# Two reorderings in the start of a fused RWKV-6 attention and GELU MLP kernel

## The chip, the cores and the metric

The kernel runs on one core of one Trainium2 chip. The metric is the device time of one execution in microseconds (us). The kernel before was timed in six runs, with a median of 612.47 us and a spread from 611.44 to 615.05 us. One of these runs, with a time of 611.57 us, was also recorded by the hardware profiler, and all views of the profile come from it. The engines are called PE (TensorE), DVE (VectorE), ACT (ScalarE), POOL (GpSimd) and SP (SyncE, which only issues DMAs here). "L648" is line 648 of the kernel.

## The reference

The reference is a recurrent attention (RWKV-6 "Finch") followed by a two-layer MLP with an exact GELU. Everything is float32.

```python
B, H, S, D = 4, 8, 768, 48
for t in range(S):                                   # attention, per batch and head
    cur = einsum('bhd,bhe->bhde', u * k_t, v_t)
    y[:, :, t] = einsum('bhd,bhde->bhe', r_t, state + cur)
    state = w_t[..., None] * state + einsum('bhd,bhe->bhde', k_t, v_t)
x = y.transpose(0, 2, 1, 3).reshape(B * S, H * D)    # 3072 x 384
h = x @ w_in                                         # 384 x 2048
g = 0.5 * h * (1 + erf(h / sqrt(2)))
out = g @ w_out                                      # 2048 x 384
```

## The kernel before, in words

The 3072 tokens are cut into eight tiles of 384 tokens (two tiles for each batch entry). For each tile the kernel computes the attention, which leaves the transposed activations of the tile in a buffer `xT`, and then the MLP of that tile, which reads `xT`. The order of all instructions on every engine is the order in which the Python code emits them; no scheduler changes it.

**Attention as a generator.** `attention(x, unit)` is a Python generator. Each `yield` ends a *slot*, and the caller decides when the next slot is emitted. Time is cut into chunks of 64 tokens. The slots of tiles 0 and 1 are: products of decays (`tot_sb`, L371); the chunk's score matrix `a_sb`, level by level, with half block sizes 1, 2, 4, 8, 16 and 32 (PE products L402 into a PSUM tile `d`, DVE multiplications of r and k by decays L437, in place, and masked copies L447); the transposed k (L566, L568); the key-value products (`kv_ps`, L592); the state chain on DVE (`st`, L606 and L617); the products of the scores with v (`y_ps`, L630), closed by a tiny DVE copy called `fence` (L634), which waits for them; the products with the states, accumulated into `y_ps` (L648); and the copies of `y_ps` into `xT`. Level 1 is split in two slots: the first emits the level's PE products alone, and the next slot emits the diagonal's PE products (L402 with `kx` as an input, two calls), then L437, L447 and the diagonal's masked copies (L413). L437 of level 1 changes r and k, which the diagonal's products read, so it waits until they are done. PSUM tiles for this work rotate through three buffers with the tag "d"; the MLP has two others.

**Head pairs and units.** The eight heads are four pairs, 0 to 3. For tile 0 the attention is cut into two *units*, which run in turns: unit 0 has pairs 0 and 1, unit 1 has pairs 2 and 3. Each head has 48 dimensions, and a pair fills 2 x 48 of the 128 partitions of `xT`. Pair 3 is laid into the partitions that the others leave free: ACT copies it into `ysb` (L672), and six small DMAs (L676, three on SP's queue and three on ACT's) move it into `xT`. Pair 2 is copied by two DVE instructions (L669). Pairs 0 and 1 are copied by two ACT instructions followed by two DVE instructions (L656).

**The end of tile 0's attention.** By L892 both units have done everything up to their key-value products, and the list of units has been reversed, so that unit 1 comes first. Unit 1 then emits its last three slots (state chain; scores times v; states and copies), and after it unit 0 the same three. `keep_warm(n)` (L190) emits n bfloat16 matmuls of zeros between slots, and they write a buffer that nobody reads.

**Weights.** The weights come as 64-bit floats and are made float32 on the chip, in 16 pieces: eight of `w_in` (two of the 16 column blocks of 128 each) and eight of `w_out` (two blocks of 128 rows each). A piece costs two ACT instructions (L291, L292) and four DVE instructions (L303, L305, L306, L310). One `convert()` emits the DVE part of a piece, and the ACT part of a piece two later.

**The MLP of tile 0 beside the attention of tile 1.** The loop at L911 runs through the steps of `mlp(0)`. Step f (0 to 15) is one block of 128 columns of `w_in`: three PE instructions (L723, `h_ps`) and a GELU on ACT (L726). Steps 16 on are the second product (L857). Between the steps it emits a `convert()` at the steps 0, 2, 4, 6, 8, 10, 12, 14, 15, 17, 18, 20, 22 and 24, and after that one slot of tile 1's attention at each step in the list `place`. In that list, the entry 1 is level 1's products, the second entry is the slot with the diagonal and the rest of level 1, the third is level 2, and so on. Later tiles use other lists and are not touched.

Of the kernel before, what the change touches and what calls it, by code (L numbers as in the profile page):

```python
# [44 lines left out]
def kernel(  # L45
# [27 lines left out]
    NP = u.shape[1]  # L73
# [20 lines left out]
    def units_of(x):  # L94
        return NPART if x == 0 else 1
# [37 lines left out]
    def load(x, dma):  # L133

        if x >= NX:
            return
        loaded[x] = [None, None]
        for i in range(3):
            if i == 1:
                load_v(x, dma)  # L140
                yield
            t = bufs[x % 2 if i == 0 else 1]
            for j in range(3):
                a = i * ALL + j * ALL // 3
                dma.dma_start(out=t[:, a:a + ALL // 3], in_=rkw[x, :, a:a + ALL // 3])
                yield
# [40 lines left out]
    def keep_warm(n):  # L187
        t = ps.tile([128, BANK], F32, name="warm", tag="mm", bufs=2) if n else None
        for _ in range(n):
            nc.tensor.matmul(t, lhsT=zeros[:, 0:128], rhs=zeros, start=True, stop=True)  # L190
# [62 lines left out]
    def make_quarter_masks():  # L253
        make_fine()
        for (h, a), m_q in m_qs.items():
            nc.vector.tensor_tensor(out=quarter[h][a], in0=s_qs[h][:, 0:m_q.shape[1]], in1=m_q, op=ALU.is_equal)
# [22 lines left out]
    def convert():  # L279
        for _ in conversion():  # L280
            pass
# [32 lines left out]
    def attention(x, unit):  # L314
# [346 lines left out]
        for b in reversed(range(np_)):  # L661
            for q in reversed(range(Q)):
                pair = parts[b] * Q + q
                y = ys[b][:, :, q * N3 * C:(q + 1) * N3 * C].rearrange("p c (i t) -> p c i t", t=C)
                if pair < NJ:
                    for z in range(2):
                        s = slice(z * G, z * G + D)
                        copy = nc.vector.tensor_copy if x == 0 else nc.scalar.copy
                        copy(out=xT[s, pair, :].rearrange("p (i c t) -> p c i t", c=2, t=C), in_=y[s])  # L669
                    continue  # L670
                ysb = wk.tile([128, T], F32, name="ysb", bufs=1)
                nc.scalar.copy(out=ysb.rearrange("p (i c t) -> p c i t", c=2, t=C), in_=y)  # L672
                for z in range(2):
                    for j in range(NJ):
                        e = z * G + j * (G - D)
                        (nc.scalar if z * NJ + j > (2 if x == 0 else 3) else nc.sync).dma_start(out=xT[z * G + D:(z + 1) * G, j, :], in_=ysb[e:e + G - D, :])  # L676
# [12 lines left out]
    def w_sums():  # L689

        sums.extend(cv.tile([128, HF, HM], F32, name="t", tag="raw", bufs=AHEAD) for _ in range(4))
        s3_sb.append(cv.tile([128, HF, 128], F32, name="s3", tag="raw", bufs=AHEAD))
        for i, (x, y) in enumerate((((0, 1), (0, 0)), ((1, 1), 0), ((1, 1), (0, 1)), ((1, 0), 1))):
            for k in range(2):
                ks = slice(k * FG, (k + 1) * FG)
                nc.vector.tensor_sub(sums[i][:, ks], w_quarter(*x, k), sums[y][:, ks] if isinstance(y, int) else w_quarter(*y, k))
                yield
# [169 lines left out]


    units = [attention(0, unit) for unit in range(units_of(0))]
    second = load_second(nc.sync)  # L870
    shares = chain(weight_in(gate=True), second, weight_in(gate=True), weight_in(gate=True))
# [17 lines left out]
    for _ in shares:  # L889
        pass  # L890
    convert()
    for unit, warm in zip(units, ((1, 2, 1), (0, 0, 5))):  # L892
        for n in warm:
            next(unit)
            keep_warm(n)
    convert()
    slots = attention(1, 0)
    next(slots)

    for x in range(1, NX):

        place = [1, 2, 4, 7, 9, 11, 13, 15, 18, 20, 26, 32] if x == 1 else [1, 6, 8, 13, 15, 16, 18, 18, 20, 21]
        place_next = [38, 47] if x == 1 else [21, 24] if x % 2 == 0 else [25, 27]
        loads = load(x + 1, nc.scalar if x > 1 else nc.sync)

        times = range(20, 30) if x == 1 else (2, 3, 4, 5, 16, 17, 18, 19, 20, 21)
        following = attention(x + 1, 0) if x + 1 < NX else iter(())
        more = iter(())  # L910
        for step, _ in enumerate(mlp(x - 1)):  # L911
            if x == 1 and step == 2 * NF - 2:

                make_quarter_masks()
                more = w_sums()
            next(more, None)
            if x == 1 and step in (0, 2, 4, 6, 8, 10, 12, 14, 15, 17, 18, 20, 22, 24):
                convert()
            if step in times:
                next(loads, None)  # L920
            while place and place[0] <= step:
                place.pop(0)
                next(slots, None)
            while place_next and place_next[0] <= step:
                place_next.pop(0)
                next(following, None)
        for _ in slots:
            pass
        slots = following
# [62 lines left out]
```

## Time and profile before

| What | Value |
|---|---|
| Median of six runs | 612.47 us (611.44 to 615.05) |
| Profiled execution | 611.57 us |
| Its span, first to last instruction | 609.8 us |
| PE busy | 593.4 us (97%) |
| DVE busy | 448.6 us (74%) |
| ACT busy | 173.3 us (28%) |
| Mean granted PE clock | 0.994 |

The granted PE clock is given as a share of full speed. All stretches named below are in us from the span's start. The attention of tile 0 takes the first 46 us or so, and the MLP's first matmul (L723) starts at 46.38 us. From there to about 119 us, tile 1's attention, tile 0's MLP and the conversion of the weights run side by side. A busy PE is not a PE at its peak, and idle time of an engine that is not the bottleneck costs nothing.

### The profile page before, as it was taken

How to read it: one execution, taken by the hardware profiler on the slowest of the kernel's cores; microseconds unless marked ns; L12 is line 12 of the kernel's file. 1: busy time of each engine (PE TensorE's matmuls, PEld its weight loads, DVE VectorE, ACT ScalarE, POOL GpSimd, SP SyncE). 2: the span in 40 equal slices, each digit the busy share in tenths (PEclk: the TensorE clock that was granted, in tenths of full speed). 3: DMA queues.
4: the chain of work that ended last, by engine and by line, in shares of the span. 5: the costliest groups of instructions: out<-in, count | busy, mean ns of one | idle time of the engine just before them, and what ended most of it. 6: DMA issues, size and time to landing. Idle time of an engine off the chain costs nothing.

```text
span 609.8 us, 15812 instructions
## 1 busy us (share of the span) xinstructions
PE 593.4 (97%) x6917; PEld 447.0 (73%) x6935; DVE 448.6 (74%) x801; ACT 173.3 (28%) x389; POOL 8.4 (1%) x24
## 2 busy tenths in 40 slices
PE   7779999999999999999999999999999999999997
PEld 4555666656699578986689568995689668995694
DVE  8959999998885978588875988679786988520120
ACT  2436367023222322203322232113222232012200
POOL 4100000000000000000000000000000000000000
PEclk9989899999999999999999999999999999999999
DMA  5775358003052205203052304213052002010001
GB/s 205 252 234 183 105 158 292 35 23 92 3 108 79 91 2 107 74 20 92 1 110 73 97 1 77 90 35 91 3 110 71 8 2 40 21 38 0 1 1 40
DMA packets 50565, 46.71 MB, mean 77 GB/s; under 512 B 31680, under 2 KB 35904, under 8 KB 50496
## 3 DMA queue, kind: packets, MB, share of 16 engines
q1 hardware_dynamic: 33152, 29.31, 15.7%
q10 hardware_dynamic: 17344, 16.39, 10.0%
q8 instruction: 55, 0.90, 0.6%
q14 instruction: 14, 0.11, 0.1%
HBM read 36.24 MB, written 4.72 MB: 67 GB/s over the span
## 4 chain that ended last, share of the span: by engine, by line
PE 92%; DVE 5%; issue 2%; DMA 1%; ACT 0%; SPq 0%; DVEq 0%
PE h_ps L723 40%; PE o_ps L743 30%; PE o_ps L857 7%; PE d L515 4%; PE y_ps L648 2%; PE kv_ps L592 2%; PE d L402 2%; PE y_ps L630 2%; PE d L508 1%; DVE rkw L437 1%; DVE tot_sb L371 1%; DMA rkw<-in_rkw_dram 1%; DVE a_sb L447 1%; PE warm L190 1%; DVE e L306 0%
## 5 line engine op out<-in xcount | busy, mean ns | idle before, releaser
L723 PE MATMUL h_ps<-xT,w_in_sb 128*128 128x384 f32 x768 | 255.8, 491 | 0.2 <-PE warm L190 0.2
L723 PEld LDWEIGHTS h_ps<-xT,w_in_sb 128*128 128x128 f32 x768 | 144.9, 191 | 98.5 <-issue 1.7
L726 ACT ACTIVATE g<-h_ps 128x384 f32<-128x384 f32 (+1 forms) x128 | 57.2, 449 | 200.5 <-PE h_ps L723 200.5
L743 PE MATMUL o_ps<-t,s 128*128 128x192 f32 x480 | 81.9, 329 | 0.0
L743 PEld LDWEIGHTS o_ps<-t,s 128*128 128x128 f32 x480 | 77.8, 190 | 0.7
L546 DVE COPY_PREDICATED a_sb<-quarter,d 128x384 f32<-128x384 uint8 (+2 forms) x108 | 45.1, 438 | 2.5
L857 PE MATMUL o_ps<-w_out_sb,g 128*128 128x384 f32 x128 | 42.7, 489 | 0.0
L743 PE MATMUL o_ps<-w_out_sb,g 128*128 128x192 f32 x224 | 38.7, 326 | 0.0
L743 PEld LDWEIGHTS o_ps<-w_out_sb,g 128*128 128x128 f32 x224 | 37.0, 190 | 1.9
L857 PEld LDWEIGHTS o_ps<-w_out_sb,g 128*128 128x128 f32 x128 | 23.9, 190 | 16.2 <-DVE o_sb L863 0.6
L736 DVE TENSOR_TENSOR s<-g 128x512 f32<-128x512 f32 x14 | 9.4, 670 | 29.1 <-ACT g L726 29.1
L743 PE MATMUL o_ps<-w_out_sb,s 128*128 128x192 f32 x160 | 28.3, 330 | 0.0
L743 PE MATMUL o_ps<-t,g 128*128 128x192 f32 x160 | 27.6, 326 | 0.0
L402 PEld LDWEIGHTS d<-rkw 64*64 64x64 f32 x1152 | 18.6, 134 | 12.0 <-DVE rkw L437 4.2
L339 DVE TRANSPOSE_TENSOR_REDUCE rkw<-kx 128x48 f32<-128x1536 f32 (+3 forms) x24 | 26.8, 1157 | 0.2
L515 PEld LDWEIGHTS d<-kx,rkw 64*64 64x64 f32 x1152 | 24.3, 133 | 3.4 <-DVE a_sb L553 1.6
L515 PE MATMUL d<-kx,rkw 64*64 64x96 f32 x1152 | 26.5, 245 | 0.0
L743 PEld LDWEIGHTS o_ps<-t,g 128*128 128x128 f32 x160 | 26.3, 190 | 0.0
L743 PEld LDWEIGHTS o_ps<-w_out_sb,s 128*128 128x128 f32 x160 | 25.9, 190 | 0.4
L402 PE MATMUL d<-rkw 64*64 64x64 f32 (+1 forms) x1152 | 20.9, 221 | 4.9 <-DVE a_sb L447 2.5
L528 DVE TENSOR_TENSOR rkw<-rkw,tot_sb 128x768 f32<-128x768 f32 x12 | 11.5, 958 | 17.4 <-PE d L515 17.4
L375 DVE TENSOR_TENSOR rkw<-rkw 128x384 f32<-128x384 f32 (+2 forms) x24 | 23.6, 1009 | 0.4
(117 smaller groups left out, 642.4 us busy)
## 6 DMA issues: line engine op xcount, KB each, us to landing
rkw<-in_rkw_dram ACTq DMA_DIRECT2D x45, 256.0 KB, 2.8
raw<-in_w_out_dram SPq DMA_DIRECT2D x8, 768.0 KB, 4.5
out_dram<-o_sb SPq DMA_DIRECT2D x21, 192.0 KB, 1.9
raw<-in_w_in_dram SPq DMA_DIRECT2D x5, 768.0 KB, 4.9
v_in<-in_v_dram ACTq DMA_DIRECT2D x5, 584.0 KB, 3.7
raw<-in_w_in_dram SPq DMA_DIRECT2D x9, 256.0 KB, 4.8
rkw<-in_rkw_dram SPq DMA_DIRECT2D x8, 288.0 KB, 3.6
rkw<-in_rkw_dram SPq DMA_DIRECT2D x9, 256.0 KB, 7.3
```

What stands on the lines that cost most here:

```text
L339: nc.vector.tensor_reduce(out=fine_sb[:, e, 0:n].rearrange("p a n -> p (a n)"), in_=kx[:, o:o + n * n_m].rearrange("p (m j) -> p m j", j=3 ...
L375: nc.vector.tensor_mul(z, z, by)
L402: nc.tensor.matmul(d[half[p], g, n * width:(n + 1) * width], lhsT=kc[half[g], b, i, p], rhs=right(half[g], b, i, p), start=True, stop=True)
L515: nc.tensor.matmul(d[half[p], g, i * 3 * C // 2:(i + 1) * 3 * C // 2], lhsT=kc[half[g], (n + i) // NI, (n + i) % NI, p], rhs=rx[half[g], 2 ...
L546: nc.vector.copy_predicated(out=an[:, :, :, :, (a + 1) * h:], mask=mask.to_broadcast(data.shape), data=data)
L592: nc.tensor.matmul(kv_ps[half[g], p, i * D:(i + 1) * D], lhsT=k_t(b, i, p, g), rhs=vs(b, i, g)[half[p], 0:D], start=True, stop=True)
L630: nc.tensor.matmul(y_ps[half[g ^ swap(b)], p, i * C:(i + 1) * C], lhsT=vs(b, i, g)[half[p]], rhs=at[half[p], g, b * NI + i, :], start=(i = ...
L648: nc.tensor.matmul(ys[b][half[g ^ swap(b)], c % 2, i * C:(i + 1) * C], lhsT=src[half[g], o:o + G], rhs=rc[half[g], b, i, c % 2], start=Fal ...
L723: nc.tensor.matmul(h_ps, lhsT=w_in_sb[:, f // FI, j, f % FI * 128:(f % FI + 1) * 128], rhs=xT[:, j, :], start=(j == 0), stop=(j == NJ - 1))
L726: nc.scalar.activation(out=gs[group][:, f % FG, 0:t], in_=h_ps[:, 0:t], func=AF.Gelu)
L743: nc.tensor.matmul(o, lhsT=lhs(j), rhs=rhs(j), start=start and j == 0, stop=(j == HF - 1), skip_group_check=True)
L857: nc.tensor.matmul(o, lhsT=block(i, f // HF, f % HF), rhs=w_out_sb[:, f, :], start=(f == 0), stop=(f == NF - 1))
```

## The change

There are two edits, both in the order of instructions.

The first concerns the end of tile 0's attention. A `yield` in front of pair 2's copies makes them a slot of their own in unit 1. The list of units and warming matmuls is written out: unit 1's three slots come as before, then unit 0's state chain, then pair 2's copies, then unit 0's other two slots. On DVE, the order "pair 2's copies, unit 0's state chain, fence" becomes "unit 0's state chain, pair 2's copies, fence". On PE the order stays, and the warming matmuls behind unit 0's last products are four instead of five.

The second concerns the beginning of tile 1's attention. The entries 2 and 4 in `place` become 3 and 5. On PE, the diagonal's products come after step 3 instead of step 2, and level 2's products after step 5 instead of step 4. The order on DVE, ACT, POOL and SP is not changed by this edit, since the conversions stay at their steps.

```diff
@@ -661,6 +661,9 @@ (in attention)
             for q in reversed(range(Q)):
                 pair = parts[b] * Q + q
+                if x == 0 and pair == NP - 2:
+
+                    yield
                 y = ys[b][:, :, q * N3 * C:(q + 1) * N3 * C].rearrange("p c (i t) -> p c i t", t=C)
@@ -889,10 +892,9 @@
     convert()
-    for unit, warm in zip(units, ((1, 2, 1), (0, 0, 5))):
-        for n in warm:
-            next(unit)
-            keep_warm(n)
+    for unit, n in ((0, 1), (0, 2), (0, 1), (1, 0), (0, 0), (1, 0), (1, 4)):
+        next(units[unit])
+        keep_warm(n)
     convert()
@@ -901,7 +903,7 @@
-        place = [1, 2, 4, 7, 9, 11, 13, 15, 18, 20, 26, 32] if x == 1 else [1, 6, 8, 13, 15, 16, 18, 18, 20, 21]
+        place = [1, 3, 5, 7, 9, 11, 13, 15, 18, 20, 26, 32] if x == 1 else [1, 6, 8, 13, 15, 16, 18, 18, 20, 21]
```

In the new list `units[0]` is unit 1, because the units are reversed. Behind the added lines the line numbers grow by three: the copies of pair 2 are L672 and the MLP's first product is L726 in the changed kernel.

## The prediction

> **What bounds the kernel now.** I read the page first: PE is busy for 97% of the span, so only the few us where it idles or runs slowly can be won, and the slices put them in the first 70 us. Next the chain of waits, from 36 to 62 us:
>
> ```profile
> 36.72 1.41 PE y_ps L648 x39
> 38.15 0.49 ACT ysb L672
> 38.67 0.55 DVE xT L669
> 39.23 0.56 DVE xT L669
> 39.80 0.27 DVE st L617
> 40.10 1.84 DVE st L606 x10
> 41.94 0.08 DVE fence L634
> 42.06 1.97 PE y_ps L648 x39
> ...
> 44.54 0.48 ACT xT L656
> ...
> 45.05 0.55 DVE xT L656
> 45.61 0.56 DVE xT L656
> ...
> 61.37 1.60 PE d L402 x96
> ```
>
> Columns: start, duration, what. Unit 1's last products, ysb, pair 2's copies, unit 0's state chain, the fence and unit 0's last products stand in one line. PE waits at its end. Third, the waits, in two answers (PE in 38 to 119 us, DVE in 46 to 116 us; total, times, longest):
>
> ```profile
> PE y_ps L648 <- DVE fence L634: 2.8, 1, 2.8
> PE d L402 <- DVE a_sb L447: 1.6, 1, 1.6
> ...
> DVE rkw L437 <- PE d L402: 0.9, 1, 0.9
> ```
>
> The third line says most. Between 46 and 116 us, DVE waits once only, for 0.9 us. In that stage DVE is the bound, not PE. Where PE catches up with it is in the timeline:
>
> ```profile
> 114.50 0.96 DVE L310 CUSTOM_DVE_ANT_0 w_out_sb<-f,e 128x1536 uint16<-128x1536 uint16 x1
> 115.51 2.39 PEld L857 LDWEIGHTS o_ps<-w_out_sb,g 128*128 128x128 f32 x8 [0.19 <-DVE w_out_sb L310]
> ```
>
> The last weight piece is converted at 115.46, and PE's weight load waits 0.19 for it. A gain by 115 us is therefore what DVE gains on its way from the end of L656 (46.17) to 115.46, whatever PE saves in between. Fourth, PE alone in stretches of 3.41 us (busy us, granted clock, DMA share, GB/s):
>
> ```profile
> 15.33:18.74 3.41, 2.50 (x98) 1.00 0.59 182
> ...
> 39.22:42.64 3.42, 0.64 (x24) 1.00 0.40 78
> 42.64:46.05 3.41, 3.19 (x32) 0.50 1.00 352
> ...
> 59.70:63.12 3.42, 1.83 (x98) 1.00 0.26 98
> 63.12:66.53 3.41, 3.41 (x6) 0.50 0.15 13
> ```
>
> After a stretch with 0.64 busy, and after one with 1.83, the clock was at half for 3.41 us; after stretches with 2.50 it was not.
>
> **The sum's base.** It is made against the profiled execution, 611.57 (span 609.8 and 1.77 around it). The median of the six runs is 0.90 above that, and I add this at the end. The changed kernel may have the same spread.
>
> **Edit 1, the DVE order.** DVE sits idle from 36.48 (end of unit 1's fence) to 38.67 (2.19, released by ACT ysb). The chain of unit 0 (L617 and ten L606, 39.80 to 41.94) takes 2.14 and needs key-value products that PE ended at 34.64. Moved ahead, it runs from 36.5 to 38.67 and fills the gap. Pair 2's copies start at about 38.70 instead of 38.67, end at 39.83, and the fence at 39.99 instead of 42.00. The fence also needs unit 0's L630, done at 39.28. So 2.00 goes. Late next is pair 2's own pair of copies, 1.12 long, which nothing shortens. If the chain did not fit the gap, every us over it would push the copies and fence by as much. The copies of pair 2 are needed by the MLP only, several us later. The moved instructions issue no DMA: the six DMAs of ysb on SP and ACT are issued at 38.66 as before, the last issue ending at 40.8 with a landing of 2.2 at most, so by 43; the first L723 needs them at 43.8 (below). The next weight pieces on SP's queue stay behind them.
>
> **Edit 1, PE.** Unit 0's L648 starts at 40.06. It took 1.94 before, because the clock fell to half at 42.6, in the middle of it; unit 1's took 1.38 at full clock. The bounds are 1.38 and twice that. Now PE idles 0.78 ahead of it (39.28 to 40.06) instead of 2.78, so I take 1.38: 0.56 more goes. The two ACT and the two DVE copies behind it (0.96 and 1.12) stay on the path. End of L656: 40.06 + 1.38 + 0.05 + 0.98 + 0.02 + 1.12 = 43.61 instead of 46.17, which is 2.56 earlier. The dropped warming matmul: the five ended with 46.23, beside L656's end, at half clock. Four at full clock (0.21 each, from two in 0.43) end at 42.3. Their removal gains nothing, but PE then idles until the first L723, from 42.3 to about 43.76, or 1.4 us. That gap is new, and it is the question of the rival below.
>
> **Edit 2, on PE.** Let A be the end of L656. From rows of before: two steps of L723 4.04 to 4.07, each slot's L402 1.53. L723 starts at A + 0.15. PE now reaches the diagonal's end at A + 0.15 + 4.04 + 1.53 + 4.07 + 1.54 = A + 11.33, level 2 at A + 15.4. Level 1's L447 ended at 61.22, A + 15.05, so the wait of 1.59 is gone, and with it the half clock behind it (63.1 to 66.5, about 1.7 lost, half of 3.41). Late next: level 4's products, at A + 21.0 on PE, wait for level 2's L437 (67.76, A + 21.59): 0.65. Level 8's, at A + 27.3, wait for level 4's L437 (74.06, A + 27.89): 0.65. Level 16's wait no more. PE starts level 8 at A + 28.0 instead of A + 30.03 (76.20): 2.0 gained on PE.
>
> **Edit 2, on DVE, which counts.** DVE's order is the same. It runs without a wait from A to 88.15 (A + 41.98), then has 0.92 of waiting for level 32's products, which end at A + 42.8. In the new order these end at A + 40.8, so the 0.92 goes, and no more than that can go, since the rest is work. PE's other 1.1 comes back as waits on the last two weight pieces, shortly before 115 us. The conversions themselves need ACT's half of the pieces, which is paced by DVE's buffers, and loads five pieces ahead, both shifted alike.
>
> A price is added too: level 1's L437 on DVE (57.59, A + 11.42) must wait for the diagonal's products. Before, these ended 1.96 earlier (55.63). Now they end at A + 11.33, that is 0.1 before. I take 0.05 lost here. But the cover is gone: any delay of PE between the first L723 and the diagonal now moves DVE, and with it the 115 us point, one for one. Behind L437 in DVE's queue stands everything of the stage. Later than that there is cover again: level 2, 4, 8 and 16 products end 2.9, 2.9, 2.2 and 2.1 ahead of the L437 that needs them.
>
> The sum: 611.57 - 2.00 - 0.56 - 0.92 + 0.05 = 608.14; plus 0.90 for the median, 609.0. From 120 us on PE is without waits in the chain but for one of 1.07 at 313 us in which it waited for nothing shown; such a stall may come or go, and I price it at nothing, with 1.07 either way in the range.
>
> **A rule against it.** The row: 1.59 us of idle PE in the stretch from 59.70 was followed by half clock. The page "TensorE: Matmul & The Clock Gate" of the Trainium skill says, in its section "HAM oscillation — how this bites in real kernels", that gaps above about 3.4 us of idle PE are to be avoided. By this rule the new gap of 1.4 us would cost nothing and the sum would stand; by the row it may cost 1.1 to 1.7 us. The trace disagrees with the rule, since both of its throttled stretches had less idle than that (2.78 and 1.59).
>
> **The rivals.**
> Half clock at the MLP's start: the new gap of 1.4 us (and 0.78 just before) makes the clock drop in steps 0 to 3, ahead of the diagonal. For it: 1.83 busy of 3.41, in small matmuls, was not enough; 2.50 was; here the stretch would have about 2.3, of which 0.9 is warming matmuls. Against it: these and L723 fill the array, unlike L402. The price is half of what PE works at half clock, from 1.15 (stretch from 42.64, of which PE works 2.3) to 1.7 (all 3.41), one for one through the diagonal: 1.4, so 610.4.
>
> Edit 2 pays nothing: if the 0.92 on DVE merely moves, to L437 of level 1 or to a conversion that waits for ACT, the time is 609.9. For it speaks that L437 stands only 0.1 behind the diagonal; against it, that DVE's order and all its other partners keep their distance.
>
> Edit 1 pays nothing, because the copies or the chain wait for something that the profile put down to ysb; then 609.0 + 2.56 = 611.6. Against it: the chain's inputs are done at 34.64.
>
> Slower than before: the half clock does not last for one stretch but stays through steps 0 to 3, because each slow stretch has a gap again. Its place is the same, its price 1.7 a stretch on the diagonal. It decides from 5.2 us on (609.0 to 614.3), that is from just over three stretches; 614.2 at three, 615.8 at four. Against it: both slow stretches in the trace were followed by full clock.
>
> **How the numbers follow.** The forecast has 57%, half clock at the start 22%, edit 2 without gain 10%, edit 1 without gain 5%, slower 6%. What a measurement here can tell from no change is 0.3%, or 1.84 us: faster is below 610.63. The six runs lie from 1.0 below to 2.6 above their median, so a median may be off by 0.7 or so. The forecast falls under 610.63 nearly always, the first rival in over half of its cases, the second mostly: 0.73 faster, 0.20 within, 0.07 slower. The range goes from 607.5 (the forecast, less 0.5 for a median nearer to the fastest run, less the 1.07 stall) to 611.7, which takes in the half clock at its dearest with a median 0.7 high, and edit 1 without gain. The likeliest case alone has 608.0 to 610.0.
>
> **What would show it.** Right: pair 2's copies start within 0.2 us of ysb's end with the chain before them; the fence about 2.0 earlier; unit 0's L648 at 1.4; first L726 at about 43.8; no wait of level 2's products, but ones of some 0.6 at levels 4 and 8; DVE without a wait from L656 to the last piece, ending near 112.1 (3.4 earlier); PE waiting there about 1 us. Wrong: clock of 0.5 in 43 to 55 us, a wait of L437 for the diagonal over 0.3, or the last piece later than 113.5.

## The result

The changed kernel takes 609.8 us (median of 21 runs, 607.91 to 612.63), the kernel before 612.76 us over all its runs by then (47 runs, 610.03 to 616.03). The ratio is 0.9947, with a 95% interval from 0.9935 to 0.9959: 0.53% faster by the ratio, and 3.0 us between the two medians. The forecast was 609.0 us.

The profiled execution of the changed kernel took 609.63 us, with a span of 607.8 us. Its page gives PE 592.0 us busy instead of 593.4, DVE 448.8 instead of 448.6, and a mean granted clock of 0.999 instead of 0.994. The work is the same; what changed is waiting and clock.

The timeline of DVE, around the fence and at level 1 (start, duration, line, operation; in brackets the idle time ahead of it):

```profile
37.08 0.16 DVE L634 COPY fence<-y_ps 128x2 f32<-128x2 f32 x1 [0.79 <-PE y_ps L630]
37.15 0.25 DVE L617 COPY st<-kv_ps 128x96 f32<-128x96 f32 x1
37.43 1.84 DVE L606 SCALAR_TENSOR_TENSOR st<-st,tot_sb,kv_ps 128x48 f32<-128x48 f32 x10
39.42 1.12 DVE L672 COPY xT<-y_ps 48x384 f32<-48x384 f32 x2
40.58 0.16 DVE L634 COPY fence<-y_ps 128x2 f32<-128x2 f32 x1
43.46 1.12 DVE L656 COPY xT<-y_ps 48x384 f32<-48x384 f32 x2 [2.72 <-ACT xT L656]
56.33 1.76 DVE L437 TENSOR_TENSOR rkw<-rkw 128x1536 f32<-128x1536 f32 x1 [0.25 <-PE d L402]
```

The state chain of unit 0 (L617, L606) fills the gap behind unit 1's fence, and pair 2's copies start at 39.42, 0.03 behind the end of ysb (38.91 to 39.39). The same instructions on PE:

```profile
40.79 1.63 PE L648 MATMUL y_ps<-rkw,st 64*64 64x64 f32 x40 [0.76 <-DVE fence L634]
42.36 1.04 PE L190 MATMUL warm<-zeros 128*128 128x512 bf16 x3
44.80 4.11 PE L726 MATMUL h_ps<-xT,w_in_sb 128*128 128x384 f32 x12 [1.40 <-ACT f L291]
```

The gap of 1.40 ahead of L726 is the one that the prediction worried about. It is put down to ACT's L291, but xT was complete only with DVE's L656, at 44.58. The clock stayed full in it. The waits of PE from 38 to 119 us, and those of DVE from 45 to 116 us (total, times, longest):

```profile
PE h_ps L726 <- ACT f L291: 1.4, 1, 1.4
PE d L402 <- DVE rkw L437: 1.3, 2, 0.7
PE y_ps L648 <- DVE fence L634: 0.8, 1, 0.8
...
DVE rkw L437 <- PE d L402: 0.2, 1, 0.2
...
```

Level 2's wait for L447 is gone. Two waits of 0.65 (levels 4 and 8) have come, as forecast. At the end of the stage PE's weight loads wait for the last weight piece:

```profile
113.07 2.23 PEld L860 LDWEIGHTS o_ps<-w_out_sb,g 128*128 128x128 f32 x8 [0.69 <-DVE w_out_sb L310]
```

**Three stretches.** Single executions can't be compared by their whole time, since they already differ before the place of the change. So each profile is cut in three: the *start* (up to ysb of tile 0), the *stage* (from ysb to tile 1's first L648, the last work that the change can shift), and the *rest*. In us, read from the timelines; "half clock" says where in the stage the granted clock was 0.5.

| Kernel | Start | Stage | Rest | Half clock |
|---|---|---|---|---|
| before | 38.15 | 81.21 | 490.44 | ahead of the MLP, and behind level 2's wait |
| before, again (e12) | 39.90 | 79.29 | 490.51 | ahead of the MLP and into its first step |
| changed | 38.91 | 77.86 | 491.03 | none |
| e1, edit 1 alone | 40.27 | 77.29 | 490.74 | none |
| e1 again (e11) | 41.00 | 77.27 | 491.03 | none |
| e2, edit 2 alone | 39.88 | 80.03 | 491.79 | ahead of the MLP and into its first step |
| e3, diagonal at step 2 | 40.48 | 77.30 | 490.72 | none |
| e4, no warming matmuls | 41.24 | 79.20 | 489.46 | in the MLP's first steps |
| e5, nine warming matmuls | 39.90 | 77.43 | 490.97 | none |
| e6, 1.11 more on DVE | 41.89 | 78.33 | 490.78 | none |
| e7, 1.36 more on PE | 40.97 | 77.98 | 489.65 | none |
| e8, copies on ACT | 40.75 | 75.05 | 490.50 | none |
| e9, pair 2's rows first | 41.59 | 77.01 | 489.60 | in the MLP's first steps |
| e10, level 2 at step 3 | 40.45 | 81.91 | 490.14 | behind level 2's wait, two stretches |

Between the two profiles that the prediction's sum compares, the stage became 3.35 us shorter (81.21 to 77.86).

**The clock of every execution.** One stretch of 3.41 us at half clock takes 3.41 x 0.5 / 610, or 0.003, off an execution's mean granted clock. The profiled executions agree with this: those with no such stretch in the table have a mean of 0.999 or 1.000, those with one 0.996 or 0.997, and those with two 0.994. The mean is on record for the executions without a profile too, so the stretches can be counted, though not where they lie:

| Kernel | Executions | No stretch | One | Two or more |
|---|---|---|---|---|
| before (beside e1 to e12) | 73 | 10 | 32 | 31 |
| changed (with the profiled one) | 22 | 21 | 1 | 0 |
| e1, edit 1 alone | 12 | 7 | 5 | 0 |
| e2, edit 2 alone | 12 | 2 | 7 | 3 |
| e3, diagonal at step 2 | 10 | 9 | 1 | 0 |
| e4, no warming matmuls | 12 | 1 | 6 | 5 |
| e5, nine warming matmuls | 12 | 12 | 0 | 0 |
| e6, 1.11 more on DVE | 12 | 10 | 2 | 0 |
| e7, 1.36 more on PE | 12 | 12 | 0 | 0 |
| e8, copies on ACT | 6 | 6 | 0 | 0 |
| e9, pair 2's rows first | 6 | 1 | 5 | 0 |

So the change does two things: it shortens the stage at full clock, and it makes half clock rare.

### The profile page after: what moved, and what is told of

It is laid out like the page before. It is cut to its first block, busy times and chain, and to the rows that moved or that the text cites. A ratio compares the mean times of both kernels' runs of the same rounds, so it can differ in the third digit from the quotient of the medians.

```text
span 607.8 us, 15810 instructions
## 1 busy us (share of the span) xinstructions
PE 592.0 (97%) x6916; PEld 446.0 (73%) x6934; DVE 448.8 (74%) x801; ACT 173.3 (29%) x389; POOL 8.3 (1%) x24
## 4 chain that ended last, share of the span: by engine, by line
PE 71%; DMA 1%; issue 0%; DVE 0%; ACTq 0%
PE h_ps L726 31%; PE o_ps L746 29%; PE d L515 4%; PE o_ps L860 2%; PE kv_ps L592 2%; PE y_ps L630 2%; PE y_ps L648 1%; DMA rkw<-kx 1%; PE d L508 1%; DVE o_sb L866 0%; ACTq L462 0%
## 5 line engine op out<-in xcount | busy, mean ns | idle before, releaser
L726 PE MATMUL h_ps<-xT,w_in_sb 128*128 128x384 f32 x768 | 254.1, 489 | 1.4 <-ACT f L291 1.4
L726 PEld LDWEIGHTS h_ps<-xT,w_in_sb 128*128 128x128 f32 x768 | 144.1, 190 | 98.5 <-ACT f L291 1.9
```

Source lines behind the costliest of these rows:

```text
L726: nc.tensor.matmul(h_ps, lhsT=w_in_sb[:, f // FI, j, f % FI * 128:(f % FI + 1) * 128], rhs=xT[:, j, :], start=(j == 0), stop=(j == NJ - 1))
```

## The experiments

### e1 and e11: edit 1 alone

```diff
 (the changed kernel)
-        place = [1, 3, 5, 7, 9, 11, 13, 15, 18, 20, 26, 32] if x == 1 else ...
+        place = [1, 2, 4, 7, 9, 11, 13, 15, 18, 20, 26, 32] if x == 1 else ...
```

> Edit 1 alone: the new DVE order at the end of tile 0's attention and four warming matmuls, with the diagonal and level 2 at their old steps 2 and 4. Theory (DVE is the bound from the end of L656 to the last weight piece): edit 1 brings the fence and L648 forward, 2.0 + 0.3 = 2.3 us as measured in the changed kernel, and the 0.9 us wait of DVE for level 32 stays; ratio to before about 0.996. The wait of level 2's products for L447 stays at some 1.6 us on PE. Rival (PE's own time counts, so that its idle 1.59 us and the half clock behind it are worth 2 us or more): edit 1 gives only 1 us, ratio 0.998.

> Edit 1 alone once more, one look at the clock behind level 2's wait of 1.6 us. If half clock after that wait depends on where the 3.41 us stretches fall, it may show here: then DVE waits for level 32 by up to 0.9 us and the stage from ysb to the last piece is up to 74.5 us; with full clock it is 73.5 and DVE has no wait.

Measured, e1: 611.2 us against 613.4, ratio 0.9975 (0.9957 to 0.9994). The interval holds the figures of the theory and of the rival, so the time decides nothing; the profile does. The waits of PE in e1, from 41.5 to 122 us:

```profile
PE d L402 <- DVE a_sb L447: 1.6, 1, 1.6
PE h_ps L726 <- ACT f L291: 1.4, 1, 1.4
PE y_ps L648 <- DVE fence L634: 0.8, 1, 0.8
```

Level 2's wait of 1.6 us is still there, and DVE has no wait at all between L656 and the last weight piece, in both profiles. The stage, 77.29 and 77.27, is 0.6 shorter than the changed kernel's in its profile (77.86) and 0.1 shorter than e5's (77.43). So the wait of 1.6 us on PE costs nothing by itself, as the theory says. But the theory's second half was wrong in these profiles: DVE's 0.9 for level 32, which I gave to edit 2, went without edit 2. What is missing in e1 is the half clock behind level 2's wait. PE in two stretches that take in the wait and what follows (busy us, granted clock, DMA share, GB/s):

```profile
56.85:60.30 3.45, 2.46 (x8) 1.00 0.87 274
60.30:63.70 3.40, 2.80 (x100) 1.00 0.03 7
```

This is not so in every execution of e1. Five of the twelve have a mean clock of 0.996 or 0.997, that is, one stretch at half clock, and they took 612.38 us on average; the seven with full clock took 610.60, or 1.8 less. In e11, a single execution of 611.07 us, the clock was full as well, and the last weight piece was done 73.53 us behind ysb's start, as its expectation has it for full clock.

### e12: the kernel before once more

> The kernel before once more, one look. If DVE's wait of 0.9 us for level 32 comes from half clock behind level 2's wait, it is there with half clock in steps 5 to 7 and not there without; the stage from L656's end to the last piece is 69.3 us in the first case and 68.2 in the second.

Measured, in a single execution: level 2's wait is 1.1 us (PE came to it later, since half clock also slowed the MLP's first step), the clock is full before and behind it, and DVE does not wait for level 32. PE from 56 to 70 us (busy us, granted clock, DMA share, GB/s):

```profile
56.00:70.00 14.00, 12.90 (x222) 1.00 0.57 171
```

From the end of L656 to the last piece it takes 68.1 us (69.3 in the first profile). So the 0.9 us went together with the half clock, and half clock after this wait is there in one execution and not in another of the same kernel. The time of this execution is 611.57 us, the same as the first's by chance: a start 1.75 longer, a stage 1.92 shorter.

### e2: edit 2 alone

```diff
 (the kernel before)
-        place = [1, 2, 4, 7, 9, 11, 13, 15, 18, 20, 26, 32] if x == 1 else ...
+        place = [1, 3, 5, 7, 9, 11, 13, 15, 18, 20, 26, 32] if x == 1 else ...
```

> Edit 2 alone: the diagonal after step 3 and level 2 after step 5, with the old DVE order and five warming matmuls. Theory (DVE is the bound): only DVE's own waiting can go, 0.9 us, less what level 1's L437 now waits for the diagonal (0.05 to 0.25): 0.7 to 0.9 us, ratio 0.9986. The last weight piece stays PE's releaser, with PE waits of about 0.7 us there. Rival (PE's time counts): the 1.59 us of waiting and the 1.7 us of half clock go from the time: 2 to 3.3 us, ratio 0.995 to 0.997.

Measured: 613.61 us against 613.4, ratio 1.0003 (0.9983 to 1.0022). The rival's 2 to 3.3 us are excluded; the theory's 0.7 to 0.9 is inside, but no gain is seen. Half clock is somewhat rarer: two stretches or more in 3 of 12 executions, against 17 of 33 of the kernel before that ran beside them. In the profile, the one wait of DVE from 47.5 to 118 us is the price that the prediction named:

```profile
DVE rkw L437 <- PE d L402: 0.6, 1, 0.6
```

The half clock ahead of the MLP reached into its first step, the diagonal was late, and level 1's L437 waited. The stage, 80.03, is 0.7 longer than that of the kernel before with full clock behind level 2 (79.29), and 1.2 shorter than with half clock there (81.21).

### e3: the diagonal back at step 2, level 2 at step 5

```diff
 (the changed kernel)
-        place = [1, 3, 5, ...
+        place = [1, 2, 5, ...
```

> The changed kernel with the diagonal back at step 2 and level 2 still at step 5. Theory (level 1's L437 stands right behind the diagonal's products and so has no cover left): its wait of 0.25 us goes, and with it 0.2 to 0.3 us of the time: ratio to before 0.0004 under the changed kernel's 0.9947, so 0.994; level 2's products still don't wait. Rival (the diagonal's place is of no weight): 0.995, no difference.

Measured: 611.14 us, ratio 0.9969 (0.9952 to 0.9987). Theory and rival, 0.994 and 0.995, both lie just outside the interval, which is too wide to see a difference of 0.25 us between them. In the profile the wait of L437 for the diagonal is gone, and DVE waits nowhere from L656 to the last piece. The stage is 77.30, 0.13 shorter than with the diagonal at step 3 and full clock (e5, 77.43). So in these profiles the diagonal's later place costs 0.1 to 0.6 us and brings nothing, and level 2's later place does not shorten the stage against e1's. It does go with fewer stretches at half clock: 1 of 10 executions here, 5 of 12 in e1. By their times, 611.14 and 611.2 us, the two can't be told apart.

### e4 and e5: the gap ahead of the MLP, wider and filled

```diff
 (the changed kernel; e4, then e5)
-    for unit, n in (..., (1, 4)):
+    for unit, n in (..., (1, 0)):
+    for unit, n in (..., (1, 9)):
```

> The changed kernel without the four warming matmuls behind unit 0's last products, so that PE idles 2.3 us instead of 1.4 ahead of the first L726. Half-clock theory (a stretch of 3.41 us in which PE works for about half or less is followed by half clock): the clock falls to 0.5 in steps 0 to 3, the diagonal is 1.1 to 1.7 us later, L437 waits for it, and the time is 1.1 to 1.7 us longer than the changed kernel's: ratio to before 0.9965 to 0.9975. Rival (gaps below 3.4 us cost nothing, as the rule weighed in the prediction has it): no difference from the changed kernel, 0.995.

> The changed kernel with nine warming matmuls instead of four in the gap ahead of the first L726. At 0.21 us each they end about 0.3 us before xT is complete. Theory: in the profiled execution the clock was full at the start of the MLP, so nothing is gained there; if a part of the executions has half clock in steps 0 to 3, the median falls by up to 0.5 us and the spread narrows: ratio 0.994 to 0.995. Rival (the matmuls end late and push the first L726, as they would at half clock): slower by up to 0.5 us.

Measured, e4: 611.93 us, ratio 0.9976 (0.9955 to 0.9998). The interval lies just above the rival's 0.995, but it meets the changed kernel's own (0.9935 to 0.9959), so the time alone hardly excludes the rival. The profile shows the chain of causes: PE idles 2.4 us, the clock falls to half for 3.4 us, in which the MLP's first steps run, the diagonal is late, and DVE waits. PE around the first L726, which starts at 46.96 (busy us, mean granted clock, DMA share, GB/s), and DVE's waits from 47 to 118 us:

```profile
46.50:50.00 3.50, 3.04 (x6) 0.69 0.89 323
50.00:52.00 2.00, 2.00 (x6) 0.69 0.82 245
...
DVE rkw L437 <- PE d L402: 1.8, 1, 1.8
```

The stage is 79.20, 1.8 longer than e5's. And it is not this execution alone: 11 of e4's 12 have at least one stretch at half clock, against 1 of 22 with four warming matmuls and none of 12 with nine. So the danger that the prediction's first rival described is real, at the price that it gave at its dearest (1.7), and four matmuls of zeros are what keeps it away. e5: 609.06 us, ratio 0.9954 (0.9934 to 0.9974), stage 77.43. Nine instead of four gain nothing that can be seen.

### e6 and e7: more work on DVE, more work on PE

```diff
 (e6)
+            if x == 1 and step in (5, 8):
+                z = w_in_sb[:, 0].rearrange("p j c -> p (j c)")
+                nc.vector.tensor_copy(out=z, in_=z)
 (e7)
+                if x == 0 and f >= NF - 2:
+                    nc.tensor.matmul(h_ps, lhsT=w_in_sb[:, f // FI, 0, f % FI * 128:(f % FI + 1) * 128],
+                                     rhs=xT[:, 0, :], start=True, stop=True)
```

> The changed kernel with two more DVE instructions in tile 0's MLP, at steps 5 and 8: each copies 128 x 768 float32 of w_in_sb onto itself, so nothing changes in the result. Their duration is read from the trace, 0.4 to 0.96 us each. Theory (DVE is the bound of this stage): the time grows by their whole sum, 0.8 to 1.9 us. Rival (PE is the bound, as its busy share of 97% suggests): less than a third of that, since PE has work to do meanwhile.

> The changed kernel with two more PE instructions, one ahead of step 14 and one ahead of step 15 of tile 0's MLP: each multiplies the step's first operands once more into h_ps, which the step's own first matmul then overwrites, so nothing changes in the result. They take 0.68 us each, 1.36 together. Theory (PE waits twice 0.7 us for the last two weight pieces, so that much of its time is free): the time is unchanged within 0.2 us, and the two waits shrink to next to nothing. Rival (PE is the bound): 1.36 us longer.

Measured, e6: the added instructions in the profile (line, count, shortest, median and longest in ns, first and last start):

```profile
L923 DVE COPY w_in_sb<-w_in_sb x2: 553/554/554, 67.3 to 79.5; 128x768 f32<-128x768 f32 x2
```

They add 1.11 us, and the stage is 0.90 longer than e5's: 81%, where the theory had all of it and the rival less than a third. The time was 610.09 us, ratio 0.9973 (0.9952 to 0.9994), which is in keeping with it. e7: of the 1.36 us added on PE, 0.55 shows in the stage (77.98), against at most 0.2 by the theory and 1.36 by the rival. The last weight piece came no later than in e5 (73.67 and 73.68 us behind ysb), so DVE was not touched; PE simply had about 0.8 us to spare there, not 1.4. The time was 610.07 us, ratio 0.9964 (0.9942 to 0.9985). Both stages are compared with e5's, which ran beside them and has full clock and no wait of L437. Against the changed kernel's own profile, in which L648 and level 1's products were slower by 0.25 and 0.2, the differences are 0.47 and 0.12. By either, more of DVE's added time shows than of PE's, and by the times alone e6 and e7 can't be told apart. So DVE is the bound of this stage, with PE less than 1 us behind.

### e8: the copies of pairs 0 and 1 on ACT alone

If DVE is the bound, its two copies into xT, and its wait for ACT's two, need not stand ahead of its weight pieces.

```diff
 (the changed kernel)
-            for c, copy in enumerate((nc.scalar.copy, nc.vector.tensor_copy)):
+            for c, copy in enumerate((nc.scalar.copy, nc.scalar.copy)):
...
-        place = [1, 3, 5, ...
+        place = [1, 2, 4, ...
```

> The changed kernel with all four copies of pairs 0 and 1 into xT on ACT (two of them were on DVE, behind ACT's two), and the diagonal and level 2 at their old steps 2 and 4. Theory (DVE is the bound, and its work from the first weight piece on need not wait for the copies): DVE starts the next weight piece at the fence, some 3.8 us earlier; the first L726 starts 0.2 us earlier (four copies of 0.48 instead of 0.96 + 1.12); level 1's L437 becomes bound by the diagonal, 2.5 us earlier than in the changed kernel; PE's four waits (two of 0.65, two of 0.7) go. The time is 2.0 to 2.7 us shorter than the changed kernel's: ratio to before 0.9905. Rival (ACT becomes the bound, its GELUs late by the 1.1 us of copies): no gain, or a PE wait for a free h_ps buffer.

Measured: 607.03 us against 612.04, ratio 0.9914 (0.9883 to 0.9945). The stage is 75.05, 2.4 shorter than e5's and 2.8 shorter than in the changed kernel's profile; the median is 2.0 below that of e5, which ran beside it. The forecast was 2.0 to 2.7. The waits from 44 to 115 us on DVE, and from 41 to 122 us on PE:

```profile
DVE rkw L437 <- PE d L402: 1.2, 1, 1.2
DVE f L303 <- ACT f L291: 0.2, 1, 0.2
...
PE h_ps L726 <- ACT xT L656: 1.1, 1, 1.1
PE y_ps L648 <- DVE fence L634: 0.8, 1, 0.8
```

All waits of PE behind the first L726 are gone. Level 1's L437 now waits for the diagonal, that is, DVE is ahead of PE. This version is faster than the kernel before by 0.55 to 1.17%, and its median is 2.8 us under the changed kernel's.

### e9: pair 2's rows first

```diff
 (e8, copies pair by pair, and no warming matmuls behind unit 0's last products)
+                if x == 0 and f < 2:
+                    if f == 0:
+                        pair_ps = [... h_ps, two tiles ...]
+                        for j in (2, 0, 1):
+                            for i in range(2):
+                                nc.tensor.matmul(pair_ps[i], lhsT=w_in_sb[:, 0, j, i * 128:(i + 1) * 128], rhs=xT[:, j, :],
+                                                 start=(j == 2), stop=(j == 1))
+                    h_ps = pair_ps[f]
```

> All copies of pairs 0 and 1 on ACT, pair by pair, the diagonal and level 2 at steps 2 and 4, no warming matmuls behind unit 0's last products; and steps 0 and 1 of tile 0's MLP start with their products of pair 2's rows, which are in xT already, then pair 0's, then pair 1's, for both steps in turns. Theory (with DVE's wait moved out of the way, the copies that stand between L648 and the first L726 are next): PE goes from L648 straight into the MLP, 1.9 us earlier than with the copies on ACT alone; step 2 waits some 0.8 us for step 0's GELU; level 1's L437 no longer waits for the diagonal: the stage from ysb to the last weight piece, 71.3 us there, becomes 70.0 to 70.4, and the time 1.0 to 1.3 us shorter: ratio to before 0.989 to 0.990. Rival (ACT, which now has the copies, the weights' first half and u times r in a row ahead of step 0's GELU, becomes the bound): no gain.

Measured: 608.62 us against 614.47, ratio 0.9902 (0.9873 to 0.9932), but the profile shows a stage of 77.01 and a wait that no theory had:

```profile
PE h_ps L729 <- DMA xT<-ysb: 2.3, 1, 2.3
```

The first product of pair 2's rows needs the last of the six small DMAs of ysb. The slowest of them landed 3.5 us after its issue in this execution (2.2 in both the first profile and the changed kernel's), and PE idled 2.3 us and went on at half clock. The last weight piece was done 73.26 us behind ysb's start, where 70.0 to 70.4 was forecast. DVE waited 1.8 us for ACT's half of a weight piece, too, but ACT had itself waited for PE's late products ahead of the first GELU. So in this execution e9's idea fails first on a DMA; whether ACT would have been the bound without that stays open. Five of the six executions have a stretch at half clock. By the time e9 can't be told from e8.

### e10: level 2 at step 3

```diff
 (the changed kernel)
-        place = [1, 3, 5, ...
+        place = [1, 2, 3, ...
```

> The changed kernel with the diagonal at step 2 and level 2 at step 3, one step earlier than in the kernel before; a weight piece comes behind level 2's work on DVE instead of ahead of it. PE then waits for L447 some 3.6 us (1.6 and one more step of 2.0). If DVE is the bound and only half clock turns PE's waiting into time: half clock follows this longer wait, DVE waits for a level's products later on by 0.5 to 1.5 us, and the stage from ysb to the last weight piece (73.6 us at full clock) becomes 74.1 to 75.1. If PE's wait itself counts: 75.6 or more. If neither counts: 73.6.

Measured, in a single execution: 614.29 us, with this wait of PE from 41 to 122 us:

```profile
PE d L402 <- DVE a_sb L447: 3.5, 1, 3.5
```

It is followed by half clock for two stretches instead of one (busy us, mean granted clock, DMA share, GB/s):

```profile
59.50:67.50 8.00, 6.44 (x102) 0.58 0.11 42
```

DVE then waits three times for a level's products, 4.0 us in all, and the stage is 81.91, 4.6 longer than e3's. From ysb to the last weight piece it takes 78.02 us. That number falls to the second case, "75.6 or more", in which PE's wait itself counts, and not to the first, 74.1 to 75.1. But the first had one stretch at half clock in view, and two came. How much of the 4.0 us is the longer wait and how much the second stretch, this execution does not show. It does show that level 2's place can cost several us on the early side.

## Why the prediction was right or wrong

**Edit 1, the DVE order: right.** From ysb's start to the fence's end it was 3.85 us in both profiles of the kernel before and 1.83 in the changed one: 2.02 gone, 2.00 forecast. e1 shows it without edit 2.

**Edit 1, L648's clock: right in kind, too large.** L648 took 1.63 instead of 1.94 in the changed kernel's profile, so 0.31 went and not 0.56; the clock was full, and a stall of PE's weight loads (0.17) sits in it. In the other profiles with the new order it took 1.38 or 1.39, as forecast. But it took 1.38 with the old order in e12 and e2, too: that 0.56 is a matter of the execution, not of the order alone.

**Edit 2, DVE's 0.92: read from one execution.** "In the new order these end at A + 40.8, so the 0.92 goes" is true of the profile shown: from the end of L656 to the last piece 0.85 went (69.29 to 68.44), where the 0.92 less the 0.05 for L437 made 0.87. But the wait of 0.92 comes with the half clock behind level 2, and not every execution has that. It is absent with the old places in e1, in e11 and in e12, and e2 shows no gain by time. With full clock on both sides, edit 2 loses about 0.1 (e5 against e1 and e3). What it does is to make the half clock rarer: of the 68 executions of the changed kernel, e3, e5, e6 and e7, which all have level 2 at step 5, 4 have a stretch of it, and of e1's 12, with level 2 at step 4, 5 have one, at a price of 1.8 us. Where these stretches lie is not recorded, but the gap ahead of the MLP is the same 1.4 us in e1 as in the changed kernel, and level 2's wait is what differs. An estimate from these counts and this price is 0.6 us on average. The prediction's step was to take a wait that some executions have as a price that all of them pay. That edit 2 gains 0.6 in the median is not shown by any run: e1 and e3 have the same time.

**The price on L437: right place, more than I took.** It waited 0.25 in the changed kernel, against 0.05, because level 1's products took 1.80 instead of 1.60 there; 0.6 in e2 and 1.8 in e4. The statement that any delay of PE between the first L726 and the diagonal moves DVE is borne out by e4.

**DVE as the bound: right.** e6 shows 0.9 of 1.11 us, and e1's profile shows 1.6 us of PE waiting that cost nothing while the clock stayed full. The free time of PE at the last two weight pieces was overestimated: 0.8 by e7, and the prediction had about 1.1.

**The first rival.** Half clock at the MLP's start did not show in the changed kernel's profile or in e5, and only 1 of the changed kernel's 22 executions has a stretch of it anywhere. With a gap 1.0 wider it did (e4), at 1.8, and 11 of 12 executions have one. The prediction gave this rival 22% on two stretches of a single trace; it had no row that could tell a harmless gap of 1.4 us from a costly one of 2.4.

**The sum.** 3.43 us were forecast for the profile's stage, and 3.35 were measured. By parts, 2.00, 0.56 and 0.87 were forecast; 2.02 went up to the fence, 0.33 from there to the end of L656, 0.85 from there to the last weight piece, and 0.15 behind it, which no term had. So L648's shortfall was partly made up by something unforeseen, and that is luck. Against the medians 3.43 was set and 3.0 found. The base was a profile with two stretches at half clock, and 31 of 73 executions of the kernel before have at least as many. At full clock behind level 2, the stage went from 79.29 to 77.43, or 1.9 us. The whole times say the same: among the executions without half clock that ran beside each other, e5's average is 609.27 us (12) and that of the kernel before 611.14 (5), 1.9 more. So of the 3.0 us about 1.9 come from edit 1's order on DVE, and the other 1.1 or so, by this estimate, are stretches at half clock that the kernel before has in 63 of 73 executions and the changed one in 1 of 22.

**The rule weighed.** The row: PE idled 1.6 (the first profile), 2.3 (e9), 2.4 (e4) and 2.8 us ahead of a half-clock stretch, and 1.4 or 1.6 without one following (the changed kernel, e1). So a gap of under 3.4 us can bring half clock. The page says which gaps to avoid; that shorter ones cost nothing is the prediction's reading of it, and the reading does not hold here. That a wait of 1.6 us has half clock behind it in one execution (the first profile) and not in others (e1 and e11) agrees with a second statement of "TensorE: Matmul & The Clock Gate" in the Trainium skill, section "What's actually happening": the clock is set by the activity in a window of about 3.4 us that runs freely and does not start with the kernel. The half-clock stretch from 63.12 to 66.53 in the first profile is 3.41 us long.

## What to carry to other kernels

Find the engine that has no waits over a whole stage, and count only what that engine gains: here 1.6 us of PE waiting were worth nothing while the clock stayed full, and 2.0 us of idle DVE were worth 1.9. A wait seen in a single profile may come from a half clock that the next execution does not have, so read a second profile, and the mean clock of the executions that have none, before giving its price to an edit. PE's idle time can still cost something by way of the clock: here four small matmuls of zeros in a gap of 2.4 us kept it full. When two pieces of work on the bounding engine can be swapped and one of them has a gap to fit in, swap them; when a copy can move to an engine with time to spare, try that too: in e8 it was worth another 2.0 to 2.4 us.

## What the runs showed of the hardware that was not expected

The time up to ysb, which no edit touches, went from 38.15 to 41.89 us in these profiles, more than the change is worth. In e6, whose start is the longest, 2.6 of the 3.7 us of difference are stalls of PE that are put down to nothing the profile shows, from 20 to 42 us:

```profile
PE y_ps L630 <- issue: 1.4, 1, 1.4
PE d L402 <- issue: 0.8, 1, 0.8
...
PE kv_ps L592 <- issue: 0.4, 1, 0.4
```

The first profile of the kernel before has none of these in that stretch. What causes them was not tried. The six small DMAs of ysb, 24 KB each, landed in 1.9 to 2.2 us in the profiles of the kernel before and of the changed kernel, and in e2, e10 and e12; in the other profiles the slowest of them took 3.3 us (e7) to 4.0 us (e3 and e8). Only in e9 does the profile show an engine that waited for one.
